# Another PSUM bank for one output tile, a single copy for the last piece, named PSUM buffers and a reordered program in a fused attention and gated-convolution kernel

## The chip, the cores and the metric

The kernel runs on one core of one Trainium2 chip. The metric is the time of one execution on the device, in microseconds (us). TensorE (PE) multiplies, ScalarE (ACT) and VectorE (DVE) do the elementwise work, SyncE (SP) issues most of the transfers. Every engine runs its own instructions strictly in the order in which they stand, and waits on semaphores for the others.

## The reference, cut to what matters

```python
# q, k, v: [8, 8, 576, 64] (batch, heads, sequence, width); p: [8, 8, 32, 64]
def sm_attn(qq, kk, vv):
    s = scale * np.matmul(qq, kk.transpose(0, 1, 3, 2))
    a = np.exp(s - np.max(s, axis=-1, keepdims=True))
    a = a / (np.sum(a, axis=-1, keepdims=True) + 1e-09)
    return np.matmul(a, vv)
p_packed = sm_attn(p, k, v)             # 32 packed queries per head
x = sm_attn(q, p_packed, p_packed)      # then laid out as [8, 576, 512]
h = np.maximum(x @ w_in, 0.0)           # w_in [512, 1024]
conv_out = sum(conv_w[t] * shifted(h, t) for t in range(3))   # along the sequence
return ((h / (1.0 + np.exp(-conv_out))) @ w_out).astype(np.float32)   # w_out [1024, 512]
```

w_in, conv_w and w_out come as 64-bit floats; the kernel turns their bits into float32 itself. The output is [8, 576, 512] in float32.

## The kernel before

**Work and names.** The attention runs in 16 groups g, each half of the heads of one batch. A group loads k, q and v (SP), transposes k and q to kT and qT (the first groups on TensorE, L568, with a copy out of PSUM on ACT or DVE, L271 and L273; later ones on DVE, L547), multiplies kT by the packed queries (S1, L588), takes the negated maximum nm (DVE, L653), the exponential a1 (ACT exp, L657), transposes a1 (PE L664, copied by ACT to a1T, L273) and multiplies it with v (AV, L673). That gives the 32 packed rows (pb, ACT L684, transposed by PE L689, copied to ppT by ACT L692). The second attention multiplies qT by ppT (S2, L588), and its softmax gives s2, transposed to a2t and split into a2hi (ACT cast, L273) and a2lo (DVE, L734). The values of the second attention times w_in are made once per batch as a product of ppT and w_in_sb (PK, L769), split into ghi (ACT cast) and glo (DVE, L805). ffn1(b, j) (L834) multiplies a2hi and a2lo by these for 128 columns of the 1024, ACT takes the relu into hbuf (L851), and the convolution and gate run over ACT (L881, tanh L891) and DVE (L883, L887, L893) into hgt. ffn2(m) treats one of 36 tiles m of 128 output rows: ACT casts hgt to xhi (L273), DVE makes the rest xlo (L987), and TensorE runs 8 chunks of three matmuls (wo_hi by xhi, wo_lo by xhi, wo_hi by xlo, L1014, 128x512 each). ACT copies the tile out of PSUM to o (L1029), and SP stores it (L1034). The last tile, m = 35, is done in pieces of columns by last_tile (matmuls L920, copies L927, L934 and L935, stores L929, L937 and L938).

**PSUM.** There are three "big" buffers of two banks each (S1, S2, transposes, PK, ffn1), and one bank each named "sm" (AV, pb, small things) and "fo" (ffn2). Most tiles of ffn2 are gathered in fo; m = 31, 33 and 35 in sm, and 30, 32 and 34 in fo.

**What sets the order.** All streams of work are generators that yield Steps (engine, estimated ns, what they take and give). A string of 1476 two-character numbers, ORDER, says which stream takes its next step; the order of an engine's instructions in the program is the order of these steps. The class Flow follows the order with estimated times; its result is used only to put filler matmuls ("idle", L251 and L256) where TensorE is expected to wait in the first part. No time that it works out changes the order.

Of the kernel before, what the change touches and what calls it, by code (L numbers as in the profile page):

```python
# [8 lines left out]
F32 = mybir.dt.float32  # L9
# [24 lines left out]
    "68674n4o4n1p2j4p4p4n1w68684l694n23661v394p284o686868681w1p6867234o684q4p23681p691w4r691p4q6969694q4p244p4r4q694p"
    "6a1w4u4q6a1p2a1w234r1p4r202a4u4q2c4s6969264s224r1p694q4s4t2a4r24691w232a1w4t6a2a6a4s6a4t686a236a4u6a4r6a4t4s234t"
    "6a4s1p2b4v4t4s4t1p1w232a696b2f6b2h1w6a276b6b1p1w1w1w6b6c2b6b6b6b6b1w1w2h4v6b1w2d6c2h4w234v6b234w296c4w6c2a6c232m"
    "4w4x6c2h4x6c2q6b4x234w4w4y6c2a4y2a4w4y236c2h6c4z4x2a236d23544x4y2h4x6d4y6c4z2a4y2a2l2o6d6d6a2a6e2a2i2e6d6d2o6d2o"
    "6d6e6d4z2a6d2o546d2r2g2i4y2a6f234z502a4z4x6e546e4z2h232k6e505050512p502323506e6e6e6e51506e6d524z6f2o2a53516e6f2a"
    "526f2a522p2t2h522h515253516f2a552o5353522v51522x2h536f2h536f6f532v6f2s2v6f516g6e56562h6f2h2y2n5657586g2h56572h6h"
    "2w586g566g566g6g6g6g566h6g306g6c59582v576g2z6h2o57582o2h57556h2w59555957582h2h2h576h6h6h2o6h325859326i2v2v582o2o"  # L40
    "596f2o5a326i5a5b595a6h596h2o2v325c6h6i5a5b6j2v5a6i2u2o6i5c5a6i336i6i2h6j5b5c6h6i2o6i5b2h6i5a5b5b5c5d5d6j2o2v6j2o"
    "5c2o5b6j5d2o326j2o5c6j5d5d5d5e5e322o5c5f5d5e6k6k2v2v6j6j2v6j6g5g6j6k2v6k6l5f6k6i6l6k6k5g6k6k6k33325h326k6l5g6m5h"
# [21 lines left out]
class Flow:  # L64
# [37 lines left out]
    def earliest(self, step, last):  # L102
        froms = [last]
# [51 lines left out]
    def run(self, order):  # L155
        for n in order:
            s = self.streams[n]
            step = s[1]
# [6 lines left out]
            for name in step.take:  # L165
                self.tokens[name].pop(0)
# [21 lines left out]
def tile_packed_attention_conv_gate(  # L188
# [11 lines left out]
    nc = tc.nc  # L200
# [898 lines left out]
```

## Time and profile before

| | |
|---|---|
| time, median of 3 runs (lowest to highest) | 400.47 us (400.37 to 400.8) |
| the profiled execution: its own time, its span | 401.49 us, 399.7 us |
| granted TensorE clock, mean | 0.999 |
| busy: PE, DVE, ACT | 391.4, 341.8, 270.0 us |
| matmuls of L1014 into fo, each of the three kinds | 248 |
| mean of one L1014 matmul (wo_hi, xhi) | 401 ns |
| bytes moved, DMA packets | 47.58 MB, 141827 |

The profile is of one execution; its time is 1.02 us over the median. Busy times are shares of the span from the first to the last instruction. A matmul's row is longer than the distance to the next one, since matmuls are pipelined; distances are read from start to start. In a row of the timeline the first number is the start in us from the start of the span, the second its length in us, and the bracket says how long the engine was idle before it and what ended that.

### The profile page before, as it was taken

Reading aid. Unit: us, or ns where it says so; the run is one execution under the profiler, and the core shown is the slowest. Engines: PE = TensorE matmul, PEld = TensorE weight load, DVE = VectorE, ACT = ScalarE, POOL = GpSimd, SP = SyncE. Lnnn points to the kernel's source line nnn. Section 1 sums busy time; section 2 is a strip of 40 time slices with the busy share of each in tenths; the row PEclk is TensorE's granted clock in tenths of the full one; section 3 lists DMA queues with packets and bytes.
Section 4 is the critical chain, followed back from the end, with each engine's and each line's share of the span. In section 5 each row is a group of like instructions: output and inputs, shape, how many; then the busy total and the mean of one; then the engine's idle time right before and its main releaser. Section 6 shows DMA issues by size and latency. Waiting matters only on the chain.

```text
span 399.7 us, 7999 instructions
## 1 busy us (share of the span) xinstructions
PE 391.4 (98%) x3275; PEld 311.7 (78%) x3275; DVE 341.8 (86%) x492; ACT 270.0 (68%) x431; POOL 2.6 (1%) x15
## 2 busy tenths in 40 slices
PE   7999999999999999999999999999999999999996
PEld 6756756688679878787788897978688788897886
DVE  4799999998999998999998999999939997876220
ACT  2799999986666669577747775767666677666121
POOL 1000000000000000000000000000000000000000
PEclk9999999999999999999999999999999999999999
DMA  8998999299568099977749548501001000000202
GB/s 278 368 373 274 197 304 159 65 159 162 164 94 112 28 120 157 178 116 125 150 81 148 153 52 172 87 2 53 28 26 54 26 29 26 28 26 2 79 26 79
DMA packets 141827, 47.58 MB, mean 119 GB/s; under 512 B 124500, under 2 KB 133076, under 8 KB 141792
## 3 DMA queue, kind: packets, MB, share of 16 engines
q1 hardware_dynamic: 141328, 46.41, 55.0%
q10 hardware_dynamic: 432, 0.66, 0.5%
q8 instruction: 25, 0.41, 0.4%
q14 instruction: 10, 0.08, 0.1%
q0 software_dynamic: 32, 0.02, 0.0%
HBM read 37.64 MB, written 9.44 MB: 118 GB/s over the span
## 4 chain that ended last, share of the span: by engine, by line
PE 83%; DMA 6%; DVE 5%; ACT 3%; SPq 1%; issue 1%; ACTq 0%; DVEq 0%
PE fo L1014 37%; PE big L834 24%; PE big L588 4%; PE big L769 3%; PE sm L1014 3%; PE sm L673 3%; PE big L964 3%; PE big L664 2%; DMA q<-in_q_dram 2%; DMA k<-in_k_dram 2%; PE big L857 2%; DMA hgt<-in_k_dram 1%; PE big L568 1%; SPq L535 1%; ACT a L657 1%
## 5 line engine op out<-in xcount | busy, mean ns | idle before, releaser
L1014 PE MATMUL fo<-wo_hi,xhi 128*128 128x512 f32 x248 | 99.6, 401 | 0.7 <-ACT o L1029 0.7
L1014 PE MATMUL fo<-wo_hi,xlo 128*128 128x512 f32 x248 | 97.0, 391 | 0.0
L1014 PE MATMUL fo<-wo_lo,xhi 128*128 128x512 f32 x248 | 96.8, 390 | 0.0
L851 ACT ACTIVATE hbuf<-big 128x576 f32<-128x576 f32 x64 | 41.9, 654 | 27.2 <-PE big L834 26.7
L1014 PEld LDWEIGHTS fo<-wo_hi,xhi 128*128 128x128 f32 x248 | 46.5, 188 | 13.4 <-issue 2.7
L987 DVE TENSOR_TENSOR xlo<-hgt,xhi 128x1024 fp32r<-128x1024 f32 (+1 forms) x38 | 41.7, 1104 | 17.9 <-ACT xhi L273 17.5
L883 DVE SCALAR_TENSOR_TENSOR hgt<-hbuf,cw,hgt 128x576 f32<-128x576 f32 x62 | 49.7, 808 | 8.0 <-ACT hgt L881 7.9
L1014 PEld LDWEIGHTS fo<-wo_hi,xlo 128*128 128x128 f32 x248 | 46.6, 188 | 10.3
L1014 PEld LDWEIGHTS fo<-wo_lo,xhi 128*128 128x128 f32 x248 | 46.7, 188 | 7.6
L891 ACT ACTIVATE hgt<-hgt 128x576 f32<-128x576 f32 x62 | 42.2, 683 | 15.4 <-DVE hgt L887 15.2
L893 DVE SCALAR_TENSOR_TENSOR hgt<-hgt,hbuf 128x576 f32<-128x576 f32 x62 | 45.9, 748 | 7.4 <-ACT hgt L891 7.1
L834 PE MATMUL big<-a2hi,ghi 128*128 128x288 f32 x224 | 50.2, 305 | 0.3 <-ACT a L657 0.3
L887 DVE SCALAR_TENSOR_TENSOR hgt<-hbuf,cw,hgt 128x576 f32<-128x576 f32 x62 | 49.6, 807 | 0.5
L881 ACT ACTIVATE hgt<-hbuf,cw 128x576 f32<-128x576 f32 x62 | 47.9, 776 | 0.9
L834 PE MATMUL big<-a2hi,glo 128*128 128x288 f32 x224 | 48.0, 295 | 0.0
L834 PE MATMUL big<-a2lo,ghi 128*128 128x288 f32 x224 | 48.0, 295 | 0.0
L834 PEld LDWEIGHTS big<-a2hi,ghi 128*128 128x128 f32 x224 | 37.6, 189 | 7.9 <-issue 1.7
L1029 ACT COPY o<-fo 128x512 f32<-128x512 f32 x31 | 18.1, 585 | 34.5 <-PE fo L1014 34.5
L273 ACT CAST xhi<-hgt 128x1024 fp32r<-128x1024 f32 (+1 forms) x38 | 36.0, 953 | 7.0 <-PE sm L1014 3.9
L834 PEld LDWEIGHTS big<-a2hi,glo 128*128 128x128 f32 x224 | 36.0, 188 | 0.0
L834 PEld LDWEIGHTS big<-a2lo,ghi 128*128 128x128 f32 x224 | 36.0, 188 | 0.0
L673 PEld LDWEIGHTS sm<-v,a1T 128*32 128x32 f32 (+1 forms) x640 | 10.3, 108 | 10.4 <-issue 4.6
(121 smaller groups left out, 542.0 us busy)
## 6 DMA issues: line engine op xcount, KB each, us to landing
out_dram<-o SPq DMA_DIRECT2D x35, 256.0 KB, 2.3
v<-in_v_dram SPq DMA_DIRECT2D x16, 512.0 KB, 5.3
k<-in_k_dram SPq DMA_DIRECT2D x48, 144.0 KB, 4.5
q<-in_q_dram SPq DMA_DIRECT2D x48, 144.0 KB, 4.0
hgt<-in_moe_w_in_dram SPq DMA_DIRECT2D x3, 1024.0 KB, 10.1
hgt<-in_moe_w_out_dram SPq DMA_DIRECT2D x3, 1024.0 KB, 7.7
hgt<-in_q_dram SPq DMA_DIRECT2D x2, 576.0 KB, 7.7
k<-in_k_dram SPq DMA_DIRECT2D x2, 576.0 KB, 9.6
```

The lines of the kernel that those rows point to most:

```text
L273: nc.scalar.copy(out=out, in_=in_)
L673: nc.tensor.matmul(out=t[32 * h : 32 * h + 32, :D], lhsT=a1T[r:, si, 32 * h : 32 * h + 32], rhs=G["v"][r:, head(g, h), si, :], start=si == ...
L834: nc.tensor.matmul(out=t[:, hf, :SH], lhsT=w[:, gg, js], rhs=x[:, hf * SH : (hf + 1) * SH], start=n == 0, stop=n == (1 if b in F1F else 3) ...
L851: nc.scalar.activation(out=inner, in_=t[:, :, :SH], func=AF.Relu, scale=0.5)
L881: nc.scalar.activation(out=d, in_=h[:, 1 : S + 1], func=AF.Copy, scale=cw[:, NJ + j : NJ + j + 1])
L883: nc.vector.scalar_tensor_tensor(out=d, in0=h[:, 0:S], scalar=cw[:, j : j + 1], in1=d, op0=ALU.mult, op1=ALU.add)
L887: nc.vector.scalar_tensor_tensor(out=d, in0=h[:, 2 : S + 2], scalar=cw[:, 2 * NJ + j : 2 * NJ + j + 1], in1=d, op0=ALU.mult, op1=ALU.add)
L891: nc.scalar.activation(out=d, in_=d, func=AF.Tanh)
L893: nc.vector.scalar_tensor_tensor(out=d, in0=d, scalar=1.0, in1=h[:, 1 : S + 1], op0=ALU.add, op1=ALU.mult)
L987: nc.vector.tensor_tensor(out=lo[:, js, o], in0=src[:, js], in1=hi[:, js, o].bitcast(F32), op=ALU.subtract)
L1014: nc.tensor.matmul(out=t, lhsT=x[:, c, :], rhs=w[:, c % 2, :], start=c + i == 0, stop=c == NJ - 1 and i == 2)
L1029: nc.scalar.copy(out=o, in_=t)
```

## The change

1. The string ORDER is another one: the same 1476 steps, of which most stand where they stood and others are moved by some places among their neighbours.
2. Flow keeps track of which of the three big buffers a step takes, and the kernel allocates that buffer by name instead of taking the next of three.
3. The two copies of qT of group 0 out of PSUM (640 and 512 columns) go from ACT to DVE.
4. w_in_sb is stored as four quarters of 256 columns, so that DVE writes each quarter as one run (L383), and the matmul of PK (L769) reads two runs of 256.
5. The last 256 columns of the last tile are copied by ACT in one instruction, where ACT and DVE took 128 each, and are stored as 64 rows by ACT's queue and 64 rows by SP's, 1 KB a row, where each stored 128 rows of 512 bytes.
6. Tile m = 29 is gathered in sm instead of fo.

```diff
 ORDER = (
-    "363636360036360703370000013470020e3405340a72050a3472050404347134343a06090505710c06050h0c0h05050c740505743b780d0b"
+    "363636360007363603007003017034020e050a72050a34340504723434047134343a050506090c710c06050h0h05050c740874053b780d05"
...
+    def take(self, n, step):
+        for name in step.take:
+            token = self.tokens[name].pop(0)
+            if name == "big":
+                self.slot = self.held[n] = token[2]
...
-    ON_DVE = {"kT00", "kT10", "kT15", "kT20", "kT25"}
+    ON_DVE = {"kT00", "kT10", "kT15", "kT20", "kT25", "qT00", "qT05"}
...
-    w_in_sb = cpool.tile([128, NCC, DFF], F32, name="w_in_sb")
+    w_in_sb = cpool.tile([128, 4, NCC, DFF // 4], F32, name="w_in_sb")
...
     def big():
-        return ps.tile([128, 2, 512], F32, name="big", tag="big", bufs=3)
+        return ps.tile([128, 2, 512], F32, name="big", tag=f"big{flow.slot}", bufs=1)
...
-            dst = w_in_sb[:, :, cols]
+            dst = w_in_sb[:, i]
...
-                    out=t[32 * c : 32 * c + 32, gg, :],
+                    out=t[32 * c : 32 * c + 32, gg, :].rearrange("c (a f) -> c a f", f=DFF // 4),
...
-                    rhs=w_in_sb[r, 2 * gg + h // 2, 512 * hf + n * p : 512 * hf + n * p + n],
+                    rhs=w_in_sb[r, 2 * hf + p : 2 * hf + p + n // 256, 2 * gg + h // 2, :],
...
-        yield Step("ACT", 250, take=["o", "o"], give=[bank])
-        n = DM // 4
-        o = [wk.tile([128, DM], F32, name="o", tag="o")[:, :n] for _ in range(2)]
-        nc.scalar.copy(out=o[0], in_=t[:, :n])
-        nc.vector.tensor_copy(out=o[1], in_=t[:, n:])
-        yield Step("SP", 600, give=["o", "o"])
-        nc.scalar.dma_start(out=rows[:, 2 * n : 3 * n], in_=o[0])
-        nc.sync.dma_start(out=rows[:, 3 * n :], in_=o[1])
+        yield Step("ACT", 340, take=["o"], give=[bank])
+        o = wk.tile([128, DM], F32, name="o", tag="o")[:, : DM // 2]
+        nc.scalar.copy(out=o, in_=t)
+        yield Step("SP", 600, give=["o"])
+        nc.scalar.dma_start(out=rows[:64, fs], in_=o[:64])
+        nc.sync.dma_start(out=rows[64:, fs], in_=o[64:])
...
-        bank = "sm" if m > NTT - 6 and m % 2 else "big" if m in SPLIT else "fo"
+        bank = "sm" if m > NTT - 8 and m % 2 else "big" if m in SPLIT else "fo"
```

TensorE's matmuls are the same but for two more fillers and for the order among neighbours. Line numbers are 8 to 10 higher in the changed kernel (L1014 is L1022, L834 is L844, L657 is L667, L547 is L557). The orders of instructions at three places follow; a row is a line, an operation, output and inputs with their buffer numbers, and the output's shape.

ACT at about 204 us of the span, where a2hi and ghi are cast and one exp (L657) is taken; before:

```order
L273 CAST xhi_2480<-hgt1_75 128x1024
L273 CAST a2hi_2498<-a2t_2496 128x576
L273 CAST ghi_2503<-big_2393 128x1024
L657 ACTIVATE a1_2514,sm1_2515<-big_2448,nm_2501 128x576
L1029 COPY o_2533<-fo_2466 128x512
L851 ACTIVATE hbuf2_78<-big_2517 128x576
```

and now, up to the cast of ghi:

```order
L283 CAST a2hi_2509<-a2t_2502 128x576
L667 ACTIVATE a1_2514,sm1_2515<-big_2451,nm_2507 128x576
L1037 COPY o_2530<-fo_2464 128x512
L861 ACTIVATE hbuf0_76<-big_2517 128x576
L891 ACTIVATE hgt0_74<-hbuf0_76,cw_72 128x576
L861 ACTIVATE hbuf1_77<-big_2545 128x576
L694 ACTIVATE pb_2568<-sm_2426,rs_2391 128x128
L283 CAST ghi_2573<-big_2396 128x1024
```

The exp and the copy of o stand ahead of the cast of ghi, which comes four instructions after them.

ACT at about 25 to 28 us, at the second attention of the first group behind the start; before:

```order
L707 ACTIVATE s2_390<-s2_390 128x576
L657 ACTIVATE a1_460,sm1_461<-big_396,nm_421 128x576
L273 COPY qT_413<-big_414 128x640
L684 ACTIVATE pb_475<-sm_435,rs_392 128x128
L273 COPY qT_413<-big_424 128x512
L692 COPY ppT_487<-sm_477 128x128
```

and now:

```order
L717 ACTIVATE s2_384<-s2_384 128x576
L283 COPY qT_413<-big_414 128x640
L283 COPY qT_413<-big_422 128x512
L667 ACTIVATE a1_473,sm1_474<-big_404,nm_428 128x576
L694 ACTIVATE pb_476<-sm_438,rs_395 128x128
L702 COPY ppT_490<-sm_481 128x128
```

The two copies of qT now stand together, ahead of exp and of pb.

DVE at about 93 to 97 us, at the transposes of a q and a k that SP loads (q in eight pieces for two groups, then k in four); before:

```order
L893 SCALAR_TENSOR_TENSOR hgt1_75<-hgt1_75,hbuf1_77 128x576
L547 STREAM_TRANSPOSE qT_1186<-q_1082 128x1152
L547 STREAM_TRANSPOSE kT_1188<-k_1132 128x1152
L883 SCALAR_TENSOR_TENSOR hgt1_75<-hbuf0_76,cw_72,hgt1_75 128x576
L883 SCALAR_TENSOR_TENSOR hgt1_75<-hbuf2_78,cw_72,hgt1_75 128x576
L887 SCALAR_TENSOR_TENSOR hgt1_75<-hbuf0_76,cw_72,hgt1_75 128x576
```

and now:

```order
L903 SCALAR_TENSOR_TENSOR hgt1_75<-hgt1_75,hbuf1_77 128x576
L557 STREAM_TRANSPOSE kT_1182<-k_1135 128x1152
L557 STREAM_TRANSPOSE qT_1209<-q_1086 128x1152
L893 SCALAR_TENSOR_TENSOR hgt1_75<-hbuf2_78,cw_72,hgt1_75 128x576
L893 SCALAR_TENSOR_TENSOR hgt1_75<-hbuf0_76,cw_72,hgt1_75 128x576
L897 SCALAR_TENSOR_TENSOR hgt1_75<-hbuf2_78,cw_72,hgt1_75 128x576
```

The transposes of k and q have changed places. On SP's queue the loads of the two q and of this k stand in the same order before and now.

More of the change, by code (lines that the diff above doesn't have):

```diff
@@ L47 @@
-    "6t6s6s6s6t6t6t6u6t6t6t6t6s6t6u6t6v6u6u6s6u6u6u6t6v6u6u6r6u6v6u6w6t6v6v6w6v6v6v6v6v6w6w6v6w6x6w6x6v6w6w6w6w6x6w6w"
-    "6u6x6x6x6x6x6x6x6x7g7g7g7g6x7g7g7g7g7g7g"
+    "363636360007363603007003017034020e050a72050a34340504723434047134343a050506090c710c06050h0h05050c740874053b780d05"
+    "0b0c0c050d0l730g0f730b050c3b050c0j0c050c3b3c0o0c0j0o0n0j763e05760c0m0j0k0c050j0c050q0i6y35750c0q0i370c0j0k3q3g0c"
+    "75050q0j0j0c0q0j050j3q0p0c6z0c0j0r0q3s3d0j3d790r0j0p3t3d0j3s3i3f0j3q0q3q0j0q770j7a770q0j3f0q0j3u3f0q3t0j3r3u3u37"
@@ L49 @@
+    "6o325m6o6o6n5q5r5n5n5p5n5n5q6p5q6p5s5q5q6p6p5p5r5r5r5r6p5s5s5q5r5r6q6p6p6p6o6p6p5s6q6p5t5t5s5p5s6q6q6q6q5q6q5t5t"
+    "6r5s5u6q5t6r5v5u6q6q5u6r5t5u5v6p5u5u6q5t6r5v6s5w5w5v5u5v6s6r6q5w5x5x6r5x6r5w6r5w5v5w6r6r5v5x6s6s6s5x5x5w5x6s6s6t"
+    "6s6s6s6r6t6t6t6u6t6t6t6t6s6t6s6t6u6v6u6u6u6u6u6u6t6v6u6r6u6v6v6v6v6t6v6v6u6w6v6w6v6v6w6w6w6w6x6x6w6w6v6w6w6w6w6x"
+    "6x6x6x6x6x6x6x6x7g6u7g7g7g7g6x7g7g7g7g7g"
 )
@@ L86, in __init__ @@
     def __init__(self, tokens, warm, busy):
-        self.tokens = {k: [(0.0, None)] * n for k, n in tokens.items()}
+        self.tokens = {k: [(0.0, None, i) for i in range(n)] for k, n in tokens.items()}
+        self.slot, self.held = 0, {}
         self.warm, self.busy = warm, busy
@@ L105, in earliest, with give @@
         froms += [self.tokens[name][step.take.count(name) - 1] for name in step.take]
-        at = max(t + self.LAG[e][step.engine] if e else 0.0 for t, e in froms)
+        at = max(t + self.LAG[e][step.engine] if e else 0.0 for t, e, *_ in froms)
         return max(at, self.free[step.engine] + (self.tail(step.tiled) if step.engine == "PE" else 0))
+    def take(self, n, step):
[3 more added lines that the diff above has]
+                self.slot = self.held[n] = token[2]
+    def give(self, n, step, end):
+        for name in step.give:
+            slot = (self.held.pop(n if n in self.held else n - 1),) if name == "big" else ()
+            self.tokens[name].append(end + slot)
+            self.tokens[name].sort(key=lambda x: x[0])
     def tail(self, tiled):
@@ L164, in run @@
                 self.table = step.table
-            for name in step.take:
-                self.tokens[name].pop(0)
+            self.take(n, step)
             if engine == "PE":
@@ L178, in run @@
                 self.free[engine] = end[0]
-            for name in step.give:
-                self.tokens[name].append(end)
-                self.tokens[name].sort(key=lambda x: x[0])
+            self.give(n, step, end)
             for event in step.sets or ():
```

45 lines of the change are left out of this document (20 added, 25 removed).

## The prediction

> **What bounds the kernel now.** I read the page first, then the waits of TensorE, then its matmul rows around each wait, and last the rows of ACT, DVE and the DMA queue at the places that the change moves. The first row below is the page's busy time by engine, the second its chain of the work that ended last. The next four are from the list of waits (who waited for whom, us in total, times, longest), and the last five are the busy time of DVE in five stretches (us busy out of the stretch, granted TensorE clock behind it).
>
> ```profile
> PE 391.4 (98%) x3275; PEld 311.7 (78%) x3275; DVE 341.8 (86%) x492; ACT 270.0 (68%) x431; POOL 2.6 (1%) x15
> ...
> PE 83%; DMA 6%; DVE 5%; ACT 3%; SPq 1%; issue 1%; ACTq 0%; DVEq 0%
> ```
>
> ```profile
> PE fo L1014 <- ACT o L1029: 0.7, 1, 0.7
> ...
> PE sm L673 <- ACT a1T L273: 0.4, 1, 0.4
> PE big L834 <- ACT a L657: 0.3, 1, 0.3
> PE sm L689 <- ACT pb L684: 0.2, 1, 0.2
> ```
>
> ```profile
> 28.00:40.00 12.00, 11.86 (x21) 1.00 0.91 289
> 40.00:60.00 20.00, 19.96 (x30) 1.00 1.13 251
> 60.00:80.00 20.00, 19.91 (x28) 1.00 0.65 113
> 80.00:94.00 14.00, 13.87 (x19) 1.00 1.42 155
> 94.00:104.00 10.00, 9.06 (x12) 1.00 0.68 152
> ```
>
> TensorE is full (98%), at full clock, and after the first microseconds its own waits come to less than 2 us. So the end moves by what the change adds to or takes from these waits, and by the tail behind the last matmul, hardly by anything else. The third list says where new waits can come from: DVE has 0.04 to 0.14 us free in each of the stretches from 28 to 94 us, so that a DVE instruction which is made to wait there pushes everything behind it, and ACT and TensorE behind that.
>
> **The change part by part.** *Tile 29 in the other bank.* TensorE begins tile 30 in the bank that ACT still copies out.
>
> ```profile
> 361.82 0.39 PE L1014 MATMUL fo<-wo_hi,xlo 128*128 128x512 f32 x1
> 362.89 0.50 PE L1014 MATMUL fo<-wo_hi,xhi 128*128 128x512 f32 x1 [0.68 <-ACT o L1029]
> 363.23 0.39 PE L1014 MATMUL fo<-wo_lo,xhi 128*128 128x512 f32 x1
> 363.46 0.40 PE L1014 MATMUL fo<-wo_hi,xlo 128*128 128x512 f32 x1
> ```
>
> ```profile
> 365.36 1.46 DVE L987 TENSOR_TENSOR xlo<-hgt,xhi 128x512 fp32r<-128x512 f32 x2
> ```
>
> Undisturbed matmuls start 0.23 apart (363.23 to 363.46). The one at 362.89 came 1.07 after its predecessor, and the next 0.34 after it: 1.07 + 0.34 - 2 x 0.23 = 0.88, with the unrounded spacing about 0.9. With tile 29 in the sm bank that stall goes: -0.9. What is late next is x of tile 31, ready at 365.36 + 1.46 = 366.8. Tile 31 begins 24 matmuls behind 362.89, near 368.4, so about 0.7 us remain when TensorE runs 0.9 ahead; and its bank, now also tile 29's, is copied out during tile 30. The gain holds. Bounds -0.9 and 0.
>
> *The last piece.* The rows are the copy of 256 columns for the piece before, the two half copies of the last piece, and their stores.
>
> ```profile
> 393.34 0.37 ACT L927 COPY o<-sm 128x256 f32<-128x256 f32 x1 [2.29 <-PE sm L920]
> ...
> 396.17 0.27 ACT L934 COPY o<-fo 128x128 f32<-128x128 f32 x1 [2.46 <-PE fo L920]
> ...
> 396.47 0.29 DVE L935 COPY o<-fo 128x128 f32<-128x128 f32 x1 [8.65 <-ACT o L934]
> ...
> 396.79 0.33 SPq L938 DMA_DIRECT2D out_dram<-o  x1
> ```
>
> DVE began when ACT's half had ended, so the store that counts left at 396.79. One copy costs 0.37 and is done at 396.54; with the 0.03 from copy to store (396.76 to 396.79) the store leaves at 396.57: -0.22. Both new stores move the same bytes in half as many rows of twice the length; no row prices that, so the landing is left alone. Bounds -0.3 and +0.1, the latter if the second store queues behind the first. The Trainium skill ("TensorEngine Tiling (Array Packing)", PSUM Bottleneck) speaks against this edit: it advises both engines for emptying PSUM. If both halves ran at once, the old form would end with the slower half, 0.29, and the new one would lose 0.08. The trace shows them one after the other, as "PSUM — Partial Sum Buffer" (PSUM bank collisions) of the Trainium skill has it for two readers of one bank and quadrant, so I keep -0.22.
>
> *The exp before the cast of ghi at 204 us.* The big buffer that L834 needs is held until exp (L657) has read it, and exp stood behind a cast.
>
> ```profile
> 203.64 1.01 ACT L273 CAST ghi<-big 128x1024 fp32r<-128x1024 f32 x1
> 204.55 0.75 ACT L657 ACTIVATE a<-big,nm 128x576 f32<-128x576 f32 x1
> ```
>
> ```profile
> 204.74 0.39 PE L1014 MATMUL fo<-wo_hi,xlo 128*128 128x512 f32 x1
> 205.44 0.53 PE L834 MATMUL big<-a2hi,ghi 128*128 128x288 f32 x2 [0.31 <-ACT a L657]
> ```
>
> Now exp starts at 203.64 and is done 0.9 earlier. L834 follows at 204.97 instead of 205.44: -0.47. I take -0.4, near that row, since the list has only tile 30's wait behind it; 0 is the other end, should DVE not keep up with a TensorE that is ahead.
>
> *The order at 26 us.* Both copies of qT now stand ahead of exp and of pb on ACT.
>
> ```profile
> 25.64 0.74 ACT L657 ACTIVATE a<-big,nm 128x576 f32<-128x576 f32 x1
> ...
> 26.37 0.68 ACT L273 COPY qT<-big 128x640 f32<-128x640 f32 x1
> 26.94 0.38 ACT L684 ACTIVATE pb<-sm,rs 128x128 f32<-128x128 f32 x1
> 27.21 0.60 ACT L273 COPY qT<-big 128x512 f32<-128x512 f32 x1
> ```
>
> The second qT copy's step, 27.21 to 27.74, now comes ahead of pb, so pb's transpose on TensorE (which waited for it, list above), S2 and L834 start about 0.55 later; the two new filler matmuls lie in that wait. DVE stays full, and TensorE meets the wait for a1T (0.4, list above) at 103 us anyway, where 0.4 of the 0.55 is lost again: +0.2, bounds 0 and +0.8. The two qT copies of group 0 that go to DVE (0.68 and 0.60 by the same rows on ACT) fall in the 1.79 us in which DVE waits for S1, which ends at 14.07: 0, and if a part of them does not fit there, it is part of the +0.8.
>
> ```profile
> 14.07 0.76 DVE L653 TENSOR_REDUCE nm<-big 128x1 f32<-128x576 f32 x1 [1.79 <-PE big L588]
> ```
>
> *kT before qT at 94 us.* DVE first, with ACT and TensorE behind it and the loads that it waits for.
>
> ```profile
> 93.64 1.37 DVE L547 STREAM_TRANSPOSE qT<-q 128x1152 f32<-128x1152 f32 x1
> 95.94 1.38 DVE L547 STREAM_TRANSPOSE kT<-k 128x1152 f32<-128x1152 f32 x1 [0.94 <-DMA k<-in_k_dram]
> 97.25 1.50 DVE L883 SCALAR_TENSOR_TENSOR hgt<-hbuf,cw,hgt 128x576 f32<-128x576 f32 x2
> ```
>
> ```profile
> 102.29 0.68 ACT L273 COPY a1T<-big 128x640 f32<-128x640 f32 x1
> ```
>
> ```profile
> 101.89 0.72 PE L588 MATMUL big<-qT,ppT 64*32 64x288 f32 x16
> 103.02 0.84 PE L673 MATMUL sm<-v,a1T 128*32 128x64 f32 x36 [0.41 <-ACT a1T L273]
> ```
>
> ```profile
> 79.40 6.84 SPq L535 DMA_DIRECT2D q<-in_q_dram  x8
> 86.34 4.36 SPq L535 DMA_DIRECT2D k<-in_k_dram  x4
> ```
>
> Before, qT ran while k was on its way, and DVE lost 0.94. Now DVE comes to kT at 93.64 and finds nothing: k is issued behind eight q pieces, as before, and lands at 95.9. DVE idles 2.3, then does both transposes; L883 starts one transpose later, 1.37. Its results run through tanh (L891) and a1T to the AV matmuls, which already waited. So TensorE's wait grows by 1.37, bounds 0 and +1.4, and nothing later gives it back.
>
> *The rest.* In two stretches S1, AV, S2 become S1, S2, AV. The rule "Mode switching requires drain" of the Trainium skill ("TensorEngine Tiling (Array Packing)", Key Properties) would give a small gain; S and AV have tile shapes of their own (64*32 and 128*32 in the rows), and I have no row for one switch: 0, bounds -0.2 and +0.1. w_in_sb by quarters and the named big buffers change neither the count nor the size of any instruction: 0; a buffer held longer would show as a wait of L834.
>
> Sum: -0.9 - 0.22 - 0.4 + 0.2 + 1.37 = +0.05. The profiled execution took 401.49 for a span of 399.7, 1.02 above the median of 400.47; I carry the difference over to the median: 400.5.
>
> **The rivals.** *Faster: k is there in time.* Should the q and k pieces leave 2.3 us earlier (the store ahead of them waits for ACT), the last term is gone: 400.5 - 1.37 = 399.1. For it: ACT's order in the whole stretch is changed, and all other terms sum to a clear gain. Against it: ahead of that store ACT's instructions are the same ones in nearly the same order. If only 1 us is saved, 0.37 stays and the time is 399.5.
>
> *Slower: the next load that is nearly late.* At 121 us DVE takes a q for which no slack was left either.
>
> ```profile
> 121.45 1.37 DVE L547 STREAM_TRANSPOSE qT<-q 128x1152 f32<-128x1152 f32 x1
> ```
>
> ```profile
> 114.14 3.51 SPq L535 DMA_DIRECT2D q<-in_q_dram  x4
> ```
>
> ```profile
> q<-in_q_dram SPq DMA_DIRECT2D x48, 144.0 KB, 4.0
> ```
>
> Four issues in 3.51 put the last near 116.8, and 4.0 later it lands: 120.8, about 0.65 before DVE wants it. In the new order the load of p stands behind a store and directly ahead of the next store and q. If that makes q 2.2 late, DVE and TensorE lose 1.5: 402.0. It decides (401.3) from 1.45 late on. Against it: two stores stand 6 us apart there, enough for p's four issues.
>
> *The bank changes nothing.* If x of tile 31 comes over 0.7 later than now against TensorE's work, it takes back what the bank gave, up to 0.9: 401.4.
>
> **How the numbers follow.** A difference of 0.2% (0.8 us, so 399.67 and 401.27) is about what a measurement of this kernel can tell from no change. Forecast, all terms as taken: 0.40. k in time, wholly or for the most part, or a smaller loss at 94 us: 0.35. A load late at 121 us or another moved reader: 0.17; the bank's gain lost: 0.08. So faster 0.35, same 0.40, slower 0.25. The range goes from 398.7 (k in time, and 0.4 from the order at 26 us and the tile shapes) to 402.0.
>
> **What would show it.** Right: no wait of a fo matmul for the out copy near 362 us; none of L834 for exp near 205; the last store 0.4 behind the last matmul's end; DVE idle 2.3 ahead of kT near 94 and an AV wait of about 1.8 near 103; pb's transpose 0.5 later near 27. The prediction is wrong if kT does not wait, or if a wait of over 0.5 stands in TensorE's list that is not named here.

## The result, and the profile after

The changed kernel took 403.15 us (median of 14 runs, 402.22 to 406.3), the kernel before on the same chip 400.85 (14 runs, 400.18 to 402.7): ratio 1.0054, 95% interval 1.0040 to 1.0068. It is slower, by 2.3 us, and outside my range. Three slow executions in what follows lie far outside the others (986.75 and 1353.83 us of the kernel before, 434.87 us of fixed), and the ratios leave them out. The profiled execution took 403.09 for a span of 401.2, at full clock. Busy times moved little; the waits tell more. First the page's busy times of the changed kernel, then its list of waits of TensorE (who waited for whom, us in total, times, longest).

```profile
PE 391.8 (98%) x3279; PEld 312.9 (78%) x3279; DVE 342.6 (85%) x493; ACT 267.8 (67%) x429; POOL 2.6 (1%) x15
```

```profile
PE fo L1022 <- ACT o L1037: 1.2, 1, 1.2
PE idle L266 <- DVE stage L252: 1.1, 1, 1.1
PE big L578 <- DMA hgt<-in_k_dram: 1.0, 1, 1.0
PE big L598 <- DVE qT L557: 0.6, 1, 0.6
PE big L598 <- ACT s L303: 0.4, 1, 0.4
PE sm L683 <- ACT a1T L283: 0.3, 1, 0.3
```

The first row (at 172 us; the one of before stood at 362 us) and the fourth are new, and I had named neither. (The second and third belong to the first microseconds, before the first k is there.)

Because both programs run the same 792 matmuls of ffn2 in full tiles (L1014, now L1022), the n-th of them can be laid against the n-th. What the changed kernel was behind, in us, at some of these matmuls, by their starts in the two profiles (at places where both have done the same work; in between, where the two orders put other matmuls first, the difference jumps by up to 3.2 and comes back):

| place in the span of before | behind | step |
|---|---|---|
| 79 us | +0.36 | (the first microseconds and the order at 26 us) |
| 108 to 151 us | +0.22 | -0.14 |
| 163 us | +1.09 | +0.87 |
| 171 us | +2.61 | +1.52 |
| 215 us | +2.22 | -0.39 |
| 360 us | +2.13 | -0.09 |
| 366 us, to the last matmul | +1.16 | -0.97 |
| end of the span | +1.55 | +0.39 |

The profiles differ by 1.6 us in time, the medians by 2.3, since the profiled execution of before stood 0.64 over its median here. Two steps, at 163 and at 171 us, make 2.4 us. Both lie close behind one place on SP's queue. These are the transfers that SP issued there, in the changed kernel and then in the kernel before.

```profile
153.21 2.96 SPq L545 DMA_DIRECT2D q<-in_q_dram  x4
156.27 0.91 SPq L510 DMA_DIRECT2D v<-in_v_dram  x1
157.22 0.61 SPq L514 DMA_DIRECT2D v<-in_v_dram  x1
158.50 5.23 SPq L545 DMA_DIRECT2D q<-in_q_dram  x4
163.84 3.54 SPq L545 DMA_DIRECT2D k<-in_k_dram  x4
167.43 1.48 SPq L1042 DMA_DIRECT2D out_dram<-o  x2
```

```profile
153.44 2.96 SPq L535 DMA_DIRECT2D q<-in_q_dram  x4
156.45 0.77 SPq L1034 DMA_DIRECT2D out_dram<-o  x1
157.31 0.39 SPq L500 DMA_DIRECT2D v<-in_v_dram  x1
...
167.59 1.40 SPq L1034 DMA_DIRECT2D out_dram<-o  x2
```

Before, the store of an output tile (m = 5) left at 156.45, between q and v. Now it stands behind v, q and k, and leaves at 167.43. There are only two buffers o, so ACT can copy the tile after the next (m = 7) out of the fo bank only when this store has landed (it landed at 171.01 by the trace, and the copy started at 171.09); the changed kernel's ACT, TensorE and DVE rows show the rest (the bracket is the idle time before, and what ended it).

```profile
171.09 0.58 ACT L1037 COPY o<-fo 128x512 f32<-128x512 f32 x1 [3.79 <-DMA out_dram<-o]
```

```profile
162.50 0.72 PE L598 MATMUL big<-qT,ppT 64*32 64x288 f32 x16 [0.63 <-DVE qT L557]
...
171.72 0.50 PE L1022 MATMUL fo<-wo_hi,xhi 128*128 128x512 f32 x1 [1.22 <-ACT o L1037]
```

```profile
160.97 1.38 DVE L557 STREAM_TRANSPOSE qT<-q 128x1152 f32<-128x1152 f32 x1 [1.87 <-DMA q<-in_q_dram]
```

In the kernel before the same copy started at 167.84, as soon as TensorE had filled the bank, and the same qT at 159.88 after 1.01 of idle time:

```profile
159.88 1.38 DVE L547 STREAM_TRANSPOSE qT<-q 128x1152 f32<-128x1152 f32 x1 [1.01 <-DMA q<-in_q_dram]
...
167.84 0.59 ACT L1029 COPY o<-fo 128x512 f32<-128x512 f32 x1 [2.17 <-PE fo L1014]
```

So the moved store cost 1.5 us, since TensorE found the fo bank uncopied. The other 0.9 us came with a q whose last piece leaves just ahead of the store's old place, where v now comes right behind it: this piece landed 5.31 us after its issue, 4.13 before. Whether the store's move made it late is taken up below.

### The profile page after: what moved, and what is told of

The parts are those of the page before. It is cut to its first block, busy times and chain, and to the rows that moved or that the text cites. A ratio compares the mean times of both kernels' runs of the same rounds, so it can differ in the third digit from the quotient of the medians.

```text
span 401.2 us, 8001 instructions
## 1 busy us (share of the span) xinstructions
PE 391.8 (98%) x3279; PEld 312.9 (78%) x3279; DVE 342.6 (85%) x493; ACT 267.8 (67%) x429; POOL 2.6 (1%) x15
## 4 chain that ended last, share of the span: by engine, by line
PE 78%; DVE 11%; DMA 5%; ACT 2%; SPq 2%; issue 1%; ACTq 0%; DVEq 0%
PE fo L1022 34%; PE big L844 21%; PE sm L1022 4%; PE big L598 3%; PE big L779 3%; PE big L972 3%; PE sm L683 2%; DVE hgt L893 2%; PE big L674 2%; SPq L545 2%; PE big L867 2%; PE big L578 2%; DVE hgt L897 1%; DMA hgt<-in_k_dram 1%; DVE hgt L903 1%; DMA q<-in_q_dram 1%
## 5 line engine op out<-in xcount | busy, mean ns | idle before, releaser
L1022 PE MATMUL fo<-wo_hi,xhi 128*128 128x512 f32 x240 | 96.4, 402 | 1.2 <-ACT o L1037 1.2
L1022 PE MATMUL fo<-wo_hi,xlo 128*128 128x512 f32 x240 | 93.9, 391 | 0.0
L1022 PE MATMUL fo<-wo_lo,xhi 128*128 128x512 f32 x240 | 93.6, 390 | 0.0
L893 DVE SCALAR_TENSOR_TENSOR hgt<-hbuf,cw,hgt 128x576 f32<-128x576 f32 x62 | 49.6, 807 | 10.4 <-ACT hgt L891 10.0
L1022 PEld LDWEIGHTS fo<-wo_hi,xhi 128*128 128x128 f32 x240 | 45.0, 188 | 13.0 <-issue 2.7
L1022 PEld LDWEIGHTS fo<-wo_hi,xlo 128*128 128x128 f32 x240 | 45.1, 188 | 10.0
L1022 PEld LDWEIGHTS fo<-wo_lo,xhi 128*128 128x128 f32 x240 | 45.1, 188 | 7.5
L844 PE MATMUL big<-a2hi,ghi 128*128 128x288 f32 x224 | 50.1, 305 | 0.0
L891 ACT ACTIVATE hgt<-hbuf,cw 128x576 f32<-128x576 f32 x62 | 47.9, 778 | 1.0
L844 PE MATMUL big<-a2lo,ghi 128*128 128x288 f32 x224 | 48.0, 295 | 0.0
L844 PE MATMUL big<-a2hi,glo 128*128 128x288 f32 x224 | 48.0, 295 | 0.0
L844 PEld LDWEIGHTS big<-a2hi,ghi 128*128 128x128 f32 x224 | 37.7, 189 | 6.6 <-issue 1.2
L844 PEld LDWEIGHTS big<-a2lo,ghi 128*128 128x128 f32 x224 | 36.0, 189 | 0.0
L844 PEld LDWEIGHTS big<-a2hi,glo 128*128 128x128 f32 x224 | 36.0, 189 | 0.0
L683 PEld LDWEIGHTS sm<-v,a1T 128*32 128x32 f32 (+1 forms) x640 | 10.3, 108 | 10.3 <-issue 6.7
```

Source lines behind the costliest of these rows:

```text
L683: nc.tensor.matmul(out=t[32 * h : 32 * h + 32, :D], lhsT=a1T[r:, si, 32 * h : 32 * h + 32], rhs=G["v"][r:, head(g, h), si, :], start=si == ...
L844: nc.tensor.matmul(out=t[:, hf, :SH], lhsT=w[:, gg, js], rhs=x[:, hf * SH : (hf + 1) * SH], start=n == 0, stop=n == (1 if b in F1F else 3) ...
L891: nc.scalar.activation(out=d, in_=h[:, 1 : S + 1], func=AF.Copy, scale=cw[:, NJ + j : NJ + j + 1])
L893: nc.vector.scalar_tensor_tensor(out=d, in0=h[:, 0:S], scalar=cw[:, j : j + 1], in1=d, op0=ALU.mult, op1=ALU.add)
L1022: nc.tensor.matmul(out=t, lhsT=x[:, c, :], rhs=w[:, c % 2, :], start=c + i == 0, stop=c == NJ - 1 and i == 2)
```

## The experiments

Behind, "the store" is this store of tile 5. Each ratio is against the kernel before on the same chip, with its 95% interval.

**The store back in its place, in the changed kernel (store_back).** The edit on SP's queue, as rows of its instructions:

```
 L545 DMA q_1897<-in_q_dram 32x36x32 x4
+L1042 DMA out_0_dram<-o_1550 128x512
 L510 DMA v_1981<-in_v_dram 128x4x256
 L514 DMA v_1981<-in_v_dram 64x4x64
 L545 DMA q_2033<-in_q_dram 32x36x32 x4
 L545 DMA k_2050<-in_k_dram 32x36x32 x4
-L1042 DMA out_0_dram<-o_1550 128x512
```

> The changed kernel with one step moved back: the store of tile 5 stands on SP's queue ahead of the load of v (group 10), as before the change, and no longer behind this v, a q and a k. Theory A (the store that was moved behind three loads makes both new waits): the wait of S2 for qT near 162 us (0.63, with its restart 0.85) and the wait of fo's matmul for the copy of o near 172 us (1.22, with its restart 1.5) both go; the time falls by about 2.3 us against the changed kernel, to about the time of the kernel before or up to 0.8 below it. Theory B (the new order on ACT and DVE around there makes the waits): both waits stay and the time stays 2 us above the kernel before.

401.01 us, ratio 0.9999 (0.9985 to 1.0014), against 1.0054 for the changed kernel. The whole list of waits of TensorE:

```profile
PE big L578 <- DMA hgt<-in_k_dram: 1.3, 1, 1.3
PE idle L266 <- DVE stage L252: 1.1, 1, 1.1
PE big L598 <- ACT s L300: 0.3, 1, 0.3
```

Both new waits are gone from the list, and the time with them. The place of this one store is the loss.

**The store behind v, ahead of q and k (store_mid).** The same edit, with the store two rows lower.

> The changed kernel with the store of tile 5 moved only half of the way back: behind v of group 10, ahead of the next q and k. Theory A1 (two mechanisms: v issued earlier delays the landing of the q before it; the late store keeps one of the two buffers of o): the wait for qT near 162 us stays (0.85), the wait of fo for the copy of o goes (1.5). Time about 1.5 us less than the changed kernel. Theory A2 (one mechanism: both waits come from the late release of o): both waits go, 2.3 us less.

401.15 us, ratio 1.0004 (0.9991 to 1.0017). The wait for the copy of o is gone. Of the wait for qT 0.3 stays:

```profile
PE big L598 <- DVE qT L557: 0.3, 1, 0.3
```

So it is q and k ahead of the store, 9 us of issuing, that hold the buffer; the wait for qT stays, smaller, with v in the store's old place. By the timed runs the held buffer is nearly all of the loss: store_mid and store_back differ by 0.05% (0.2 us), within either interval, where I had expected 0.85 us.

**The same move in the kernel before (store_late).** There the k load ahead of the store also had to stand one place earlier.

```
-L1034 DMA out_0_dram<-o_1552 128x512
 L500 DMA v_1979<-in_v_dram 128x4x256
 L504 DMA v_1979<-in_v_dram 64x4x64
 L535 DMA q_2032<-in_q_dram 32x36x32 x4
 L535 DMA k_2074<-in_k_dram 32x36x32 x4
+L1034 DMA out_0_dram<-o_1552 128x512
```

> The kernel before with two steps moved: the load of k of group 13 comes earlier among TensorE's steps of tile 9, and the store of tile 5 behind v10, q9 and this k13, as in the changed kernel. Nothing else is changed. Theory A: both waits appear (S2 for qT near 162 us, fo for the copy of o near 172 us) and the time rises by about 2.3 us, 0.6%. Theory B: no wait appears, and the time is that of the kernel before within 0.5 us.

403.42 us (6 runs), ratio 1.0060 (1.0043 to 1.0077): the loss appears by the move alone. ACT's copy again waited for the landing, and TensorE's waits for copies of o came to 2.3, of which 0.7 is the one at 362 us that this kernel has anyway:

```profile
171.08 0.59 ACT L1029 COPY o<-fo 128x512 f32<-128x512 f32 x1 [5.22 <-DMA out_dram<-o]
```

```profile
PE fo L1014 <- ACT o L1029: 2.3, 2, 1.6
```

The wait for qT, which I had expected with it, did not appear. So the store's place does not make that wait by itself. In the order of the kernel before, the last q piece landed 3.63 to 4.13 after its issue in seven profiles with the store right behind it, and 4.44 here, with v behind it. In the changed order it took 3.82 to 5.02 in six profiles with the store behind it, and 4.94 to 5.38 in four with v behind it. The difference between the two orders shows in the trace's DMA packets. In the trace a transfer has landed when the last of sixteen updates of its semaphore has come. In seven of the ten profiles of the changed order the sixteenth came 0.7 to 1.3 after the fifteenth; in the other eleven it came at most 0.1 after it. In all ten, and in none of the eight of the old order, a packet of 16 KB on the queue that the page names "instruction" was under way while this q was. So the late landing is one late part out of sixteen, beside an instruction packet. It came in all four profiles with v right behind q and in three of six with the store there. That v makes it likelier, and that the packet is its cause, are not shown.

**kT ahead of qT, in the kernel before (k_first, k_first2).** The two DVE rows at 94 us are exchanged:

```diff
-L547 STREAM_TRANSPOSE qT
 L547 STREAM_TRANSPOSE kT
+L547 STREAM_TRANSPOSE qT
```

> The kernel before with kT (group 7) transposed ahead of qT (group 5) on DVE near 94 us, and nothing else. The step of the prediction: DVE idles 2.3 us there, the AV matmuls near 103 us wait 1.8 us instead of 0.4, and the time rises by 1.37 us. Rival C (when k lands depends on which other loads share the DMA engines with it, and here it lands about 1 us earlier, as in the changed kernel): DVE idles 0.8 to 1.3 us ahead of kT, and the time rises by 0 to 0.4 us.

402.79 us (12 runs), ratio 1.0028 (1.0008 to 1.0048), but its profiled execution took 401.14, with DVE idle 0.44 ahead of kT where I had expected 2.3, and no AV wait. So I took a second profile.

> A second look at the kernel before with kT transposed ahead of qT near 94 us. The first look was the fastest of its 12 runs, whose median was 1.5 us above it. Theory D (when the last piece of k lands varies from run to run by about 1 us, and the profile showed an early one): here k lands later than 94.5, DVE idles 1 to 2.3 us and AV waits 0.8 to 1.8. Theory C (with kT first k always lands early): idle 0.2 to 0.8 again.

401.12, DVE idle 1.01 ahead of kT. Two profiles without a loss and timed runs with one: the two did not fit, and it took the last runs below to see why.

**The changed kernel once more (after2).**

> A second look at the changed kernel. The wait of fo for o near 172 us should stand again (1.0 to 1.6), since the store that it hangs on is held by SP's order. The wait of S2 for qT near 162 us, if it is a matter of when the load happens to land, may be anywhere from 0 to 1. DVE's idle time ahead of kT near 94 us: theory D 0.8 to 2.3, theory C 0.8 or less.

403.72 us in one run. TensorE waited 1.6 for the copy of o and 0.3 for qT, and DVE was idle 0.24 ahead of kT: the loss at the fo bank repeats, that at 163 us is smaller, and the one at 94 us is absent again.

**The last piece and the bank alone (t_rows, t_cols, t_one).** All three are the kernel before with tile 29 in sm and one ACT copy; the stores differ:

```diff
# t_rows, as in the changed kernel
+        nc.scalar.dma_start(out=rows[:64, fs], in_=o[:64])
+        nc.sync.dma_start(out=rows[64:, fs], in_=o[64:])
# t_cols, as before
+        nc.scalar.dma_start(out=rows[:, 2 * n : 3 * n], in_=o[:, :n])
+        nc.sync.dma_start(out=rows[:, 3 * n :], in_=o[:, n:])
# t_one
+        nc.sync.dma_start(out=rows[:, fs], in_=o)
```

> The kernel before with tile 29 in sm and with the new last piece (one copy of 256 columns by ACT, then two stores of 64 rows, one by ACT's queue and one by SP's), nothing else. The prediction's terms: the wait of fo for o near 363 us goes (-0.9 at the last matmul), and the last store is issued 0.7 behind the last matmul's start instead of 0.93 and lands as soon after its issue as before (1.66), so the end comes 2.4 behind the last matmul's start: -0.22, in all -1.1. Rival (two stores issued at the same moment take longer, as in the changed kernel's profile): issue rows of 0.54 instead of 0.33, landing 2.0 to 2.3 after issue, and the end 3.0 behind the last matmul's start: +0.4, in all -0.5.

> The kernel before with tile 29 in sm and one copy of 256 columns by ACT, but stored in two halves of 128 columns and 128 rows each (the shapes of the kernel before), both issued when the one copy is done. If it is the same moment that makes the two stores slow: issue rows near 0.5, landing 2.0 or more, as t_rows. If it is the shape (64 rows of 1 KB): issue 0.33, landing 1.7, end 2.4 behind the last matmul's start.

> Kernel before with tile 29 in the sm bank, and the last 256 columns of the last tile copied by ACT in one instruction (0.37 us) and stored by SP alone, 128 rows of 1 KB. Theory 'shape of the store' (64-row stores of 1 KB rows issue in 0.54 us and land after 2.0 to 2.3 us, while 128-row stores of 512 bytes issue in 0.33 and land after 1.7 to 1.9): a 128-row store of 1 KB rows, as the piece before it has (L929, landing 1.7), issues in about 0.33 and lands in about 1.7, so the span ends 3.6 behind the start of the last matmul (before 3.8, changed kernel 4.2), and the kernel is 1.15 us faster than before (bank 0.95, tail 0.2): ratio 0.997. Rival 'the 1 KB rows are what costs': the landing is 2.0 or more, the end 3.9 or later behind the last matmul, ratio 0.9980 or above.

t_rows 400.28 us, ratio 0.9983 (0.9970 to 0.9996); t_cols 400.33, 0.9986 (0.9970 to 1.0002); t_one 400.35, 0.9983 (0.9960 to 1.0006). All have the bank's gain; between them the times can't tell. The profiles can: first the tail of the changed kernel, then the list of transfers (KB each, us from issue to landing) of the changed kernel, of before, of t_cols and of t_one.

```profile
397.02 0.28 PE L930 MATMUL fo<-wo_hi,xlo 128*128 128x256 f32 x1
397.33 0.37 ACT L943 COPY o<-fo 128x256 f32<-128x256 f32 x1 [2.46 <-PE fo L930]
397.73 0.54 SPq L946 DMA_DIRECT2D out_dram<-o  x1
397.73 0.56 ACTq L945 DMA_DIRECT2D out_dram<-o  x1
```

```profile
out_dram<-o SPq DMA_DIRECT2D x1, 64.0 KB, 2.0
out_dram<-o ACTq DMA_DIRECT2D x1, 64.0 KB, 2.3
```

```profile
out_dram<-o ACTq DMA_DIRECT2D x1, 64.0 KB, 1.6
out_dram<-o SPq DMA_DIRECT2D x1, 64.0 KB, 1.7
```

```profile
out_dram<-o SPq DMA_DIRECT2D x1, 64.0 KB, 1.7
out_dram<-o ACTq DMA_DIRECT2D x1, 64.0 KB, 1.9
```

```profile
out_dram<-o SPq DMA_DIRECT2D x1, 128.0 KB, 3.3
```

The stores left 0.71 behind the start of the last matmul (397.02 to 397.73), 0.22 earlier than before, as predicted. But 64 rows of 1 KB take 0.54 and 0.56 to issue and 2.0 and 2.3 to land, where 128 rows of 512 bytes take 0.33 to 0.38 and 1.6 to 1.9. In t_cols both stores also leave at one moment, so it is the shape and not the simultaneity. The span ended 3.81 behind the start of the last matmul before, 4.20 in the changed kernel, 4.20 in t_rows and 3.79 in t_cols. For t_one I had expected 1.7; its one profile has 3.3 and an end 5.21 behind. The packets in its trace tell why. Of its 128 rows 120 had moved by 397.0 us; the last eight started at 397.77 and later, when an instruction packet (from 396.29 to 397.78) was over (the row of that queue for 395.6 us to the end: packets, MB, share of 16 engines):

```profile
q8 instruction: 1, 0.02, 2.0%
```

For the rest, t_one is like 128 rows of 512 bytes: 0.33 to issue, and the first packet 0.8 after the issue (0.8 to 1.0 there, 1.2 and 1.5 with 64 rows). So it is the 64 rows that cost, most of it ahead of the first packet, and the rival I had named (the 1 KB rows cost) falls. The piece before the last, 128 rows of 1 KB in every kernel, agrees: it landed in 1.69 to 1.70 in the six profiles that have no instruction packet beside it, and in 2.07 to 2.71 in the twelve that have one. "DMA: Bandwidth & Descriptors" of the Trainium skill (Why a DMA increments its semaphore by 16 and not by 1) would spread 64 rows and 128 rows over the same 16 engines, which gives no difference between the shapes. The trace has sixteen closing packets of 4 bytes for either shape, in agreement, and yet differs by 0.4 us, so the number of engines at least does not tell this price.

**Three parts taken back (fixed), and one of them put in again (fixed_k).** fixed is the changed kernel with the store of tile 5 and the qT/kT order as before, and the last stores as in t_cols.

> Changed kernel with three parts taken back: the store of tile 5 again ahead of the two v loads, the q load and the k load; qT ahead of kT at 94 us; the last piece stored as 128 rows of 512 bytes by each of two queues (still one ACT copy). Left of the change are the bank, the rest of the order, the two qT copies on DVE, w_in by quarters and named buffers. Theory (the store's place, and the 64-row stores, are all that made the kernel slower; the qT/kT order at 94 us is worth about 0): no wait of a fo matmul for the copy of o near 172 us, none over 0.35 for qT near 162; span end 3.8 behind the last matmul's start; about 1 us faster than before (bank -0.95, start +0.25, exp at 204 us 0 to -0.4): ratio 0.9965 to 0.998. Rival (kT first costs 1.4 as I predicted): this kernel is then 1.4 + 0.4 faster than the changed kernel with the store taken back, which measured 0.9999 of before: ratio 0.9955, and 1.4 below fixed_k.

400.81 us, ratio 0.9985 (0.9967 to 1.0004), just above the 0.9965 to 0.998 that I had expected. TensorE's waits are those of the first microseconds alone. The expectation of the next kernel describes another edit than the one I made: in the stretch of ORDER that I put back stands the store of tile 5, not kT. So fixed_k differs from fixed in the place of the store, with qT ahead of kT in both.

> The same as fixed, with kT ahead of qT at 94 us as in the changed kernel: the two differ in the place of one DVE instruction alone, and run on the same chip. Prediction's term: 1.37 us slower than fixed (0.34%). Theory of the profiles so far (the last k piece lands 1 to 2 us sooner after its issue when kT stands first, so that L893 starts at the same time either way): within 0.4 us (0.1%) of fixed. The timed runs of the kernel before with kT first (+0.28%) speak for something between, 1.1 us.

402.21 us, ratio 1.0019 (1.0003 to 1.0035): 1.4 us above fixed on one chip. From its list of waits, and the copy of ACT:

```profile
PE fo L1023 <- ACT o L1038: 1.2, 1, 1.2
```

```profile
170.43 0.59 ACT L1038 COPY o<-fo 128x512 f32<-128x512 f32 x1 [3.76 <-DMA out_dram<-o]
```

Laid against fixed matmul by matmul, it loses 0.64 at 162 us and 1.49 at 172 us, and nothing at 94 to 103 us (at 80 us it was 0.79 ahead of fixed, whose 128x128 matmuls at 7.5 to 10.8 us took 399 ns on average in its profile and 277 in this one, so that the spans differ by 1.6 alone). Meant for the other question, it is the cleanest pair on the held buffer: one store, one chip, and 1.49 us in the profiles beside 1.4 in the timed runs. (At 162 us its matmuls of S2 waited 0.40, which the trace puts down to ACT's L891; the late qT was done 0.14 before they began.)

**qT earlier (q_early).** In the kernel before, qT stands three DVE instructions earlier, apart from kT.

> Kernel before with qT of the group at 94 us moved up by three DVE instructions, ahead of nm, and kT behind L893: DVE's stream transposes then stand apart, and qT is over well before the k load is under way to its end. Theory X (k's last piece lands later while DVE runs a stream transpose: 5.8 to 6.2 us from issue to landing with qT directly ahead of kT, 4.1 to 4.8 with kT first): the last k piece lands 4.1 to 4.8 us after its issue, near 94.5 to 95.0. Rival Y (the landing is set by what else the queues carry at that moment, not by DVE): 5.7 to 6.2, near 95.9. The time itself: within 0.3 us of before plus what nm's 1.4 us later start costs ACT's exp; no theory rests on it.

401.85 us (10 runs), ratio 1.0014 (0.9994 to 1.0034). The last k piece landed 4.46 after its issue, which fits theory X. But in fixed and fixed_k, where qT runs directly ahead of kT, it took 4.46 and 4.90. Theory X falls.

**kT ahead of qT again, on one chip (fixed_kf, fixed2), and with k loaded first (k_load, fixed_kf2).** fixed_kf is fixed with the two transposes exchanged; fixed2 is fixed. k_load is fixed_kf with the loads exchanged too:

```
 L545 DMA q_1068<-in_q_dram 32x36x32 x4
-L545 DMA q_1086<-in_q_dram 32x36x32 x4
-L545 DMA k_1135<-in_k_dram 32x36x32 x4
+L545 DMA k_1086<-in_k_dram 32x36x32 x4
+L545 DMA q_1135<-in_q_dram 32x36x32 x4
```

> Kernel 'fixed' (store of tile 5 ahead of the loads, 128-row last stores) with kT ahead of qT at 94 us: one pair of DVE instructions exchanged, nothing else. Prediction's term: 1.37 us slower than fixed on the same chip (0.34%), DVE idle 2.3 ahead of kT. Theory of the profiles (DVE comes to the first transpose 14.3 us after the first q piece was issued, the last k piece lands 14.4 to 15.3 after it in nine of the profiles, so that kT first loses 0.2 to 1.0 on DVE, and TensorE's wait at 103 us hides about 0.5 of it): 0 to 0.4 us slower than fixed (0 to 0.1%). The timed runs of the kernel before with kT first (+0.28%): 1.1 us slower.

> Kernel 'fixed' once more, on the chip on which fixed_kf runs, as its partner: 0.9985 of before again if the store of tile 5, the last stores and the qT order are what made the changed kernel slower; the last k piece lands 14.9 us after the first q piece, DVE does not wait for it; if kT's price is 1.1 to 1.4, fixed_kf stands 0.3% above it.

fixed_kf 401.4 us, ratio 1.0011 (0.9990 to 1.0032); fixed2 400.5, 0.9981 (0.9968 to 0.9995). The two profiles lie within 0.16 us of each other at every full-tile matmul of ffn2, yet the runs do not: of fixed_kf six took 399.66 to 401.15 and six 401.64 to 403.45, of fixed2 eleven took 399.94 to 401.20 and one 402.22.

> Kernel fixed_kf (kT ahead of qT at 94 us) with the two loads exchanged as well: SP issues the four k pieces ahead of the four q pieces. fixed_kf's timed runs fall into two halves (399.7 to 401.2 and 401.6 to 403.5), fixed's do not. Theory 'the last load lands at one of two times' (14.4 to 15.3, or 15.4 to 16.8 us after the first of these loads was issued; DVE comes to the transposes at 14.3, so that kT first loses up to 2.3 when it is late, and qT first at most 0.9, part of it hidden at 103 us): with k loaded first, kT waits for nothing, qT stands where kT stood in fixed, and the upper half goes: median 400.5 to 400.8, 0.998 of before, 0.5 to 1 us under fixed_kf. Rival (kT ahead of qT costs by itself, whatever lands when): the median stays with fixed_kf's, near 401.4.

> fixed_kf once more as the partner of k_load on one chip. Theory: two halves again, the upper one 1.2 to 2.3 above the lower, median 401 to 402. Rival (the spread of fixed_kf was chance): median near 400.5 and no second half.

k_load 399.94 us, ratio 0.9972 (0.9958 to 0.9986), 0.6 under what I had expected; fixed_kf2 401.26, 0.9991 (0.9975 to 1.0008), its twelve runs from 399.77 to 402.97 without the gap between two halves that I had expected. And the profile of fixed_kf2 caught a long run (402.68). Its DVE row, its AV row on TensorE and the landing of its last two k pieces; then the landing of the same pieces in fixed_kf (399.98):

```profile
97.12 1.38 DVE L557 STREAM_TRANSPOSE kT<-k 128x1152 f32<-128x1152 f32 x1 [1.61 <-DMA k<-in_k_dram]
```

```profile
105.46 0.84 PE L683 MATMUL sm<-v,a1T 128*32 128x64 f32 x36 [1.11 <-ACT a1T L283]
```

```profile
k<-in_k_dram SPq DMA_DIRECT2D x2, 144.0 KB, 5.9
```

```profile
k<-in_k_dram SPq DMA_DIRECT2D x2, 144.0 KB, 4.9
```

This is the chain that I had predicted (k late, DVE idle ahead of kT, a1T late, AV waits 1.1), and it happens in some executions only. In 17 profiles that load k last, the last piece lands 4.1 to 4.9 us after its issue in eleven and 5.75 to 6.4 in six, with nothing between. (store_late and t_cols are among the six, t_rows among the eleven; both values occur with qT first, 4.46 in fixed and 6.03 in fixed2, and with kT first, 4.72 in fixed_kf and 5.82 in fixed_kf2.) In the six late ones fifteen of the sixteen updates had come by 4.9, and the sixteenth came 1.0 to 1.5 after them. With qT first the late landing left DVE idle for 0.3 to 1.2 (0.94 in before, 1.22 in t_one); with kT first it costs all of it. In k_load kT waits for nothing, and qT finds q there in its profile:

```profile
93.97 1.37 DVE L557 STREAM_TRANSPOSE kT<-k 128x1152 f32<-128x1152 f32 x1
95.27 1.33 DVE L557 STREAM_TRANSPOSE qT<-q 128x1152 f32<-128x1152 f32 x1
```

So kT first does not cost by itself; the rival falls. That the long runs of these kernels are late landings is shown in part, by one traced run. Laid against fixed2's, this run was 1.37 behind at 80 us already, and lost 1.04 at the AV matmuls. The 1.37 are something else. TensorE's granted clock was 0.5 for 3.4 us there (the column of 0.50; TensorE's busy time and matmuls come first):

```profile
8.00:11.00 3.00, 3.00 (x26) 1.86 (x25) 1.44 (x4) 1.00 (x3) 0.00 (x0) 0.50 0.98 373
```

In fixed2 it was 1.00 there. Among the runs with a granted clock of 0.998 or more fixed_kf still stands 1.1 above fixed2, and fixed_kf2 1.3 above k_load, so the recorded clock does not make that difference; that late landings make it in the untraced runs I infer. Why the landing has two values stays open: an instruction packet was under way beside the last piece in all seventeen profiles, so its presence alone does not tell them apart. k_load also beats both kernels: 0.28% under before, which the changed kernel exceeds by 0.54%.

## Why the prediction was wrong, point by point

**The step that failed: SP's queue.** I listed for the order at 26 us, at 94 us and at 204 us what moved on ACT, DVE and TensorE, and for SP only the queue near 121 us. The store of tile 5, moved past v, q and k at 156 us, was in the order of SP's instructions and not in my sum, which put it at nothing without a reason; with two buffers o it is a wait of ACT and then of TensorE. At the fo bank it measured +1.52 in the profile (1.4 to 1.8 in all four that have it), and in timed runs 1.4 us in the pair fixed and fixed_k and 0.55%, 2.2 us, between the ratios of the changed kernel and store_back. The step of +0.87 at 163 us, which I had not named either, is a late landing of q that the store's place may have made likelier. Other stores and loads stand elsewhere on SP's queue too; none of them shows as a wait or a step. My closing condition (a wait over 0.5 in TensorE's list that is not named) is met twice.

**kT before qT at 94 us, +1.37: mis-sized.** I took the landing at 95.9 in one profile for a fixed time. That profile had the late of two landings. In the changed kernel's profile k landed early (4.66 after its issue, where it had taken 6.19), and DVE lost 0.79, not 2.3:

```profile
94.93 1.38 DVE L557 STREAM_TRANSPOSE kT<-k 128x1152 f32<-128x1152 f32 x1 [0.79 <-DMA k<-in_k_dram]
...
97.50 1.50 DVE L893 SCALAR_TENSOR_TENSOR hgt<-hbuf,cw,hgt 128x576 f32<-128x576 f32 x2
```

L893 started at 97.50, 0.25 behind before, less than the kernel was behind already. The term is about 0 in the early case. In the late one it is 1.04 at the AV matmuls: fixed_kf2 was 1.37 behind fixed2 ahead of them and 2.41 behind it after them; the medians of fixed_kf and fixed2 differ by 0.9 us. The rival "k is there in time" came near the event in this profile, by luck and not by its reason: nothing left earlier (the last piece of k was issued 0.52 later than before), it landed sooner.

**Tile 29: right.** Predicted -0.9, measured -0.97, and -0.9 to -1.0 in every kernel with this edit. The last matmul into sm and the first of tile 30 into fo stand at undisturbed distance:

```profile
363.96 0.39 PE L1022 MATMUL sm<-wo_hi,xlo 128*128 128x512 f32 x1
364.18 0.39 PE L1022 MATMUL fo<-wo_hi,xhi 128*128 128x512 f32 x1
```

**The last piece: the issue right, the landing wrong.** -0.22 at the issue, as predicted; I left the landing alone for want of a row, and it took 0.6 more on the later of the two queues (2.28 against 1.66). Instead of -0.22 the tail gave +0.39, beyond my bound of +0.1, which had only thought of a second store behind the first. The advice of the Trainium skill that I weighed there ("TensorEngine Tiling (Array Packing)", PSUM Bottleneck: both engines for emptying PSUM) is not what decided: the copy was as fast as I had said.

**exp at 204 us: right in this pair by luck, too large in general.** -0.4 predicted, -0.39 measured, no wait of L844 left. But the old order of ACT in other kernels costs less than in the profile of before: in t_rows L834 starts 0.40 behind the matmul ahead of it, 0.17 more than undisturbed; in k_first it is 0.21, and in the five other profiles with this order at most 0.02.

```profile
204.64 0.39 PE L1012 MATMUL fo<-wo_hi,xlo 128*128 128x512 f32 x1
205.04 0.53 PE L834 MATMUL big<-a2hi,ghi 128*128 128x288 f32 x2
```

The stall of 0.47 that I had priced was that of one execution; the term is between 0 and 0.47, and mostly near 0.

**The order at 26 us: right, and smaller.** pb's transpose came at 27.84 instead of 27.38, 0.46 later; the AV matmuls ahead of the place were 0.16 late already (25.87 instead of 25.71), so the order cost 0.30 (predicted 0.55). At 108 us 0.22 of both was left (predicted 0.2). The fillers in that wait are four matmuls (27.13, 0.71 us together), not two. The copies of qT on DVE fitted where I had put them: DVE still waited 0.48 for S1 behind them.

**The rest: 0, as far as it can be told.** The table of matmuls shows no step between 108 and 151 us, and -0.09 between 215 and 360 us; the tile shapes in another sequence and w_in by quarters, if they cost or gain anything, lie within that. The rival at 121 us did not occur: DVE took that q without a wait (at 121.70).

With the two steps at 163 and 171 us at 2.4 and kT at 0 to 1.0 in place of 1.37, the tail at +0.39 and the rest as predicted, my sum becomes -0.9 + 0.39 - 0.4 + 0.2 + 2.4 = +1.7 in an execution with an early landing, against +1.55 in the profiles. Since 2.4 and 0.39 are read from these same two profiles, this only shows that no further term is missing there.

## What to carry to other kernels

A store holds its buffer until it lands, so with two buffers a store that is moved behind loads on its queue is a wait of the copy two tiles later: go through the DMA queue's order row by row, and ask of each moved store who needs its buffer. Price a transfer's landing by several executions, not by one profile; where the consumer stands within the spread of the landing, put the consumer of the earlier load first, or load first what is consumed first. When a profile and the timed runs do not agree, look at the runs one by one and profile a long one too: one profile shows one case of a wait.

## What the runs showed of the hardware

- A load of 144 KB behind two others on one queue landed 4.1 to 4.9 us after its issue in eleven profiles and 5.75 to 6.4 in six; one and the same program showed both (4.46 and 6.03 for fixed and fixed2, 4.72 and 5.82 for fixed_kf and fixed_kf2). In the late ones one of sixteen parts came 1.0 to 1.5 us after the others.
- A store of 64 rows of 1 KB took 0.54 to 0.57 us to issue and 2.0 to 2.3 to land; one of 128 rows of 512 bytes, the same bytes, 0.33 to 0.38 and 1.6 to 1.9.
- A store of 128 rows of 1 KB landed in 1.69 to 1.70 us in six profiles, and in 2.07 to 2.71 in the twelve in which the trace has an instruction packet of 16 KB beside it.
- In six of eighteen profiles matmuls of 128x128 at 7.5 to 10.8 us took 372 to 417 ns on average, and 276 or 277 in the other twelve; in four of the six the trace records a granted TensorE clock of 0.5 there, and in the other two no clock before 10.3 us. The first full-tile matmul of ffn2 started at 80.4 to 81.0 us in the six and at 79.3 to 79.9 in the twelve.
